# Output projection and down products as products of 64 rows in an attention and feed-forward kernel

## The chip, the cores and the metric

The kernel runs on one core of a Trainium2 chip. Its time is device microseconds for one execution; the median of several executions counts.

The engines are named as the profile names them: PE is TensorE's products, PEld its weight loads, DVE is VectorE, ACT is ScalarE, POOL is GpSimd, and SP is SyncE, which here issues nearly all DMAs.

## The reference

For 2048 tokens of width 576, an attention branch (32 heads of 18) is gated by a feed-forward branch (hidden width 4608):

```python
x = A_x                                         # 1 x 2048 x 576
xn = layernorm(x)
q, k, v = split_heads(xn @ wqkv)                # 32 heads of 18
s = softmax(q @ k.T * 18 ** -0.5) @ v @ wo
g = silu((gelu(xn @ w_gate) * (xn @ w_up)) @ w_down)
out = x + s * g
```

All inputs and the output are float32.

## The kernel before

**Precision.** Operands of the large products are split in a high and a low part (`split`), and a product is the sum of three: high by high, high by low, low by high.

**Stages.** A first stage normalizes and transposes x and projects q, k and v. The rest is one long loop of *sections*, 144 in all: the feed-forward branch goes over 4 blocks of 512 tokens (`b`), in each over 18 groups (`r`) of 2 x 128 hidden columns, and one section is one such set of 128 columns. Nine sections (`FIRST`) come before the attention proper, 128 run beside it (`ATT`), and the last seven after it.

**A section** (`section`, `gate_up`) has 27 pairs of products for the gate and the up projection. A pair is two products of 64 rows by 512 columns, one on the upper and one on the lower 64 rows of the array, into two banks, `pg` and `pu` (L388). Spread between them are 16 pairs of the attention, each with one product of scores (`pe`, L729) and one of the maxima that the softmax needs (`pm`, L698), on opposite halves as well. ACT takes the exponential of `pe` (L730), DVE reduces `pm` (L699).

**Behind a section** come, on PE in the order of the program text: the products with the values (`acc`, L764, 128 rows by 32 columns, 16 of them, which the profile shows as 32), sometimes a small transposition of the maxima (`max_end`, L712), a group of the output projection (`project_o`, L582, `po`, 14 products of 128 rows and 288 columns), and down products (`down`, L426, `py`, 128 rows and 288 columns, 6 to a result). `activate` makes the hidden values from `pg` and `pu` (L401 to L409), and `finish` splits them (`hh`, `hl`) and queues the group's down products in `FF["down"]` as two halves of 24, for token tiles 0, 1 and 2, 3. `downs` runs what is due. Inside the attention, both halves of most groups fall due together (`once`), as a run of 48 behind the next group's first section. DVE adds each result to `Y` (L432), or ACT copies it there in a block's first group (L430).

The output projection of a block is 8 groups, one every second section, always in front of a run of 48. DVE multiplies its result with the gate (L584), POOL adds x (L585), and SP stores it in the next section.

**Banks.** The 8 banks of PSUM go by tag: two `f` (`pg`, `pu`), three `m` (`pm`, `acc`, `po`), three `s` (`pe`, and `py` in turn).

**Order.** PE runs in the order of the text. The other engines' queues are ordered by a planner, save where `keep_in_program_order` pins an instruction. In the nine lead sections SP loads keys in chunks of 12 DMAs (`load_k`, L662), pinned, beside the weights of the next section (`load_gu`, L114), which POOL splits (`split_gu`, `wh` L94, `wl` L96).

Of the kernel before, what the change touches and what calls it, by code (L numbers as in the profile page):

```python
# [8 lines left out]
F32 = mybir.dt.float32  # L9
F32R = mybir.dt.float32r  # L10
AF = mybir.ActivationFunctionType
ALU = mybir.AluOpType
# [5 lines left out]
P = 128  # L18
# [19 lines left out]
G = 2  # L38
# [28 lines left out]
def kernel(ctx: ExitStack, tc: tile.TileContext, x, wqkv, wo, w_gate, w_up, w_down, out):  # L67
# [20 lines left out]
    identr = const.tile([P, P], F32R, name="identr")  # L88
    nc.gpsimd.tensor_copy(identr, ident)
    all_t = slice(0, TB)  # L90


    def split(hi, lo, raw, keep=lambda i: i):
# [47 lines left out]
    with tc.tile_pool(name="pro", bufs=1) as pro, tc.tile_pool(name="pps", bufs=1, space=PSUM) as pps:  # L141
# [156 lines left out]
        def after(what, before):  # L298
            tc.add_manual_dep(what.ins, before.ins.name, mybir.DependencyInfo(
                mybir.DependencyClass.Sync, mybir.DependencyReason.DATA), reason="VectorE alone on the first x")  # L300

        raw_v, ahead_qk, QR = [], [], []
        t = ORDER[0]
        c0 = slice(t * P, (t + 1) * P)
# [28 lines left out]
        for b in range(NB):  # L333
# [37 lines left out]
    ps = ctx.enter_context(tc.tile_pool(name="ps", bufs=1, space=PSUM, reuse_waits="tile"))  # L371


    FF = {"w": ahead, "xd": XD, "down": [], "gates": [], "n": 0,
          "Y": ffn.tile([P, TB // P, D], F32, name="Y")}
    finals = []

    def gate_up(tag):

# [32 lines left out]
            nc.vector.tensor_tensor(t1, t1, pu, op=ALU.mult)  # L412
        return t1

    def down(b, r, hs, wd, Y, js):
        for j in js:
            tt = slice(j * P, (j + 1) * P)
            for c in range(2):
                cc = slice(288 * c, 288 * c + 288)
                tag = "sf"[c if b == NB - 1 and r == NR - 1 else 0]  # L420
                py = ps.tile([P, 288], F32, name="py", tag=tag, bufs=BANKS[tag])
                n = 0
                for g in range(G):
                    hh, hl = hs[g]
                    for a, w in ((hh, wd[0]), (hh, wd[1]), (hl, wd[0])):
                        nc.tensor.matmul(py, a[:, tt], w[:, g, cc], start=(n == 0), stop=(n == 3 * G - 1))  # L426
                        n += 1
                yy = Y[:, j, cc]
                if r == 0:
                    nc.scalar.activation(yy, py, AF.Copy)  # L430
                else:
                    nc.vector.tensor_tensor(yy, py, yy, op=ALU.add)  # L432
                if b == NB - 1 and r == NR - 1:
                    finals.append((Y, j, c))
        if b < NB - 1 and r == NR - 1:
            FF["gates"] += [(b, j, c, Y) for j in js for c in range(2)]

# [44 lines left out]
        FF["act"] = activate(pg, pu, n < ATT.stop)  # L482

    def downs():
        while FF["down"] and (FF["down"][0][-1] < FF["n"] or FF["n"] == NF):
            down(*FF["down"].pop(0)[:-1])
            if FF["down"] and FF["gates"]:
                gates()

    def finish(pool=ffn, cut=split, bufs=1):  # L490

        n = FF["n"] - 1
        b, r = divmod(n // G, NR)
        hh = ffn.tile([P, TB], F32R, name="hh", bufs=G + 1)
        hl = ffn.tile([P, TB], F32R, name="hl", bufs=G + 1)
        cut(hh, hl, FF["act"])
        FF["hs"].append((hh, hl))
        if n % G == G - 1:
            wd = FF.pop("wd", None)
            if not wd:  # L500
                wd = [pool.tile([P, G, D], F32R, name=m, bufs=bufs) for m in ("dh", "dl")]
                cut(*wd, FF["rawd"])
            for h in range(2):
                once = n in ATT and n + G in ATT and r != NR - 2
                FF["down"].append((b, r, FF["hs"], wd, FF["Y"], (2 * h, 2 * h + 1), n + 1 + (0 if once else h)))
# [5 lines left out]
    OG = {}  # L511
    HIND = TB // P - 1

    def load_o(b, k, pool=op, heads=range(H)):
# [58 lines left out]
    def project_o(b, i, S2=None, o=None, ow=OW):  # L573
        c, j = divmod(i, TB // P)
        cc = place(b, i)[1]
        if b < NB - 1:
            xx, yy = OG["xy"]
        po = ps.tile([P, TB], F32, name="po", tag="m", bufs=3)
        o = o or OG["o"]
        terms = [(k, x, w) for k in range(KT) for x, w in ((0, 0), (0, 1), (1, 0))] + [(KT, 0, 0), (KT, 0, 1)]  # L580
        for m, (k, x, w) in enumerate(terms):
            nc.tensor.matmul(po[:, 0:288], o[x][:, k, :], ow[w][:, k, :], start=(m == 0), stop=(m == len(terms) - 1))  # L582
        if b < NB - 1:
            nc.vector.scalar_tensor_tensor(yy, yy, 0.25, po[:, 0:288], op0=ALU.mult, op1=ALU.mult)  # L584
            nc.gpsimd.tensor_tensor(yy, yy, xx, op=ALU.add)  # L585
            OG["y", b, i] = yy
        elif S2 is not None:
            nc.scalar.activation(S2[:, j], po[:, 0:288], AF.Copy)
        return po[:, 0:288]

# [10 lines left out]
    def tasks(n, part):  # L601
        for t in todo.pop((n, part), []):
            t()
# [37 lines left out]
    with tc.tile_pool(name="att", bufs=1, reuse_waits="tile") as att:  # L641
# [293 lines left out]
```

## Time and profile before

| | |
|---|---|
| median of 3 executions | 2584.83 us (2584.62 to 2585.79) |
| the profiled execution's own time | 2584.62 us |
| its span, first to last instruction | 2582.7 us |
| granted clock of TensorE | 1.000 |
| PE busy | 2575.9 us |
| DVE, ACT, POOL busy | 2010.5, 1502.5, 1389.8 us |
| products of py (L426) | 3 x 1152 |

Busy time of PE counts overlapping products once and holds their fill, so it does not say how close PE is to its best. The distance from the start of one product to the start of the next does; the chain in order of time gives it, since a piece in that chain lasts until the next piece begins. In the timeline a product's length is its time through the array (0.3 to 0.5 us), several times the distance to the next one.

### The profile page before, as it was taken

Reading aid. Unit: us, or ns where it says so; the run is one execution under the profiler, and the core shown is the slowest. Engines: PE = TensorE matmul, PEld = TensorE weight load, DVE = VectorE, ACT = ScalarE, POOL = GpSimd, SP = SyncE. Lnnn points to the kernel's source line nnn. Section 1 sums busy time; section 2 is a strip of 40 time slices with the busy share of each in tenths; the row PEclk is TensorE's granted clock in tenths of the full one; section 3 lists DMA queues with packets and bytes.
Section 4 is the critical chain, followed back from the end, with each engine's and each line's share of the span. In section 5 each row is a group of like instructions: output and inputs, shape, how many; then the busy total and the mean of one; then the engine's idle time right before and its main releaser. Section 6 shows DMA issues by size and latency. Waiting matters only on the chain.

```text
span 2582.7 us, 56466 instructions
## 1 busy us (share of the span) xinstructions
PE 2575.9 (100%) x20982; PEld 1959.8 (76%) x20982; DVE 2010.5 (78%) x3501; ACT 1502.5 (58%) x2715; POOL 1389.8 (54%) x1506
## 2 busy tenths in 40 slices
PE   9999999999999999999999999999999999999999
PEld 8888777777777777777777777777777777777778
DVE  5326888888887888888888888888888888888445
ACT  3223466666666666565667765556666765566642
POOL 2117554554566465556457565555455755555553
PEclk9999999999999999999999999999999999999999
DMA  8866443344455444544445444445445543545342
GB/s 265 267 237 162 117 104 98 102 105 105 105 135 131 110 114 105 136 111 113 127 114 133 119 125 112 125 112 133 108 109 126 141 114 104 139 110 137 78 117 59
DMA packets 394912, 326.93 MB, mean 127 GB/s; under 512 B 107980, under 2 KB 308684, under 8 KB 394640
## 3 DMA queue, kind: packets, MB, share of 16 engines
q1 hardware_dynamic: 394640, 323.32, 47.3%
q8 instruction: 168, 2.75, 0.5%
q14 instruction: 104, 0.85, 0.1%
HBM read 269.79 MB, written 52.88 MB: 125 GB/s over the span
## 4 chain that ended last, share of the span: by engine, by line
PE 99%; DVE 1%; DMA 0%; POOL 0%; ACT 0%; issue 0%; SPq 0%; DVEq 0%
PE pg L388 25%; PE py L426 18%; PE acc L764 18%; PE pu L388 10%; PE pe L729 9%; PE pm L698 9%; PE po L162 7%; PE po L582 2%; DVE mx L699 0%; PE pt L223 0%; PE pm L712 0%; DMA xx<-in_A_x_dram 0%; DVE bs L191 0%; POOL wh L94 0%; DVE m L706 0%
## 5 line engine op out<-in xcount | busy, mean ns | idle before, releaser
L730 ACT ACTIVATE pT<-pe 128x512 f32<-128x512 f32 x2048 | 1151.6, 599 | 678.4 <-PE pm L698 578.7
L699 DVE TENSOR_REDUCE mx<-pm 128x1 f32<-128x512 f32 x2048 | 1260.0, 683 | 76.4 <-PE pm L698 73.1
L388 PE MATMUL pg<-xd,wh 64*128 64x512 f32 x2592 | 935.5, 393 | 0.0
L388 PE MATMUL pu<-xd,wh 64*128 64x512 f32 x2592 | 935.1, 393 | 0.0
L698 PE MATMUL pm<-KS,q 64*128 64x512 f32 x2048 | 785.2, 388 | 0.2 <-DVE accs L770 0.2
L729 PE MATMUL pe<-q,KS 64*128 64x512 f32 x2048 | 777.9, 387 | 0.0
L94 POOL TENSOR_SCALAR wh<-raw 128x384 fp32r<-128x384 f32 x432 | 228.3, 529 | 610.2 <-PE pu L388 264.0
L388 PEld LDWEIGHTS pg<-xd,wh 64*128 64x128 f32 x2592 | 476.2, 184 | 98.5 <-issue 19.9
L388 PE MATMUL pg<-xd,wl 64*128 64x512 f32 x1296 | 502.0, 387 | 0.9 <-POOL wl L96 0.9
L388 PE MATMUL pu<-xd,wl 64*128 64x512 f32 x1296 | 501.8, 387 | 0.0
L388 PEld LDWEIGHTS pu<-xd,wh 64*128 64x128 f32 x2592 | 477.1, 184 | 22.6
L764 PE MATMUL acc<-pT,VS 128*32 128x512 f32 x4096 | 466.0, 595 | 0.0
L96 POOL TENSOR_TENSOR wl<-raw,wh 128x384 fp32r<-128x384 f32 x432 | 442.1, 1024 | 34.1
L698 PEld LDWEIGHTS pm<-KS,q 64*128 64x128 f32 x2048 | 375.7, 184 | 38.6 <-DVE mx L699 4.9
L729 PEld LDWEIGHTS pe<-q,KS 64*128 64x128 f32 x2048 | 370.1, 184 | 29.9
L432 DVE TENSOR_TENSOR Y<-py,Y 128x288 f32<-128x288 f32 x544 | 248.1, 457 | 161.1 <-PE py L426 160.8
L426 PE MATMUL py<-dh,hh 128*128 128x288 f32 x1152 | 346.0, 300 | 0.0
L426 PE MATMUL py<-dh,hl 128*128 128x288 f32 x1152 | 339.8, 295 | 0.0
L426 PE MATMUL py<-dl,hh 128*128 128x288 f32 x1152 | 339.6, 295 | 0.0
L764 PEld LDWEIGHTS acc<-pT,VS 128*32 128x32 f32 x4096 | 120.5, 109 | 274.5 <-issue 271.2
L388 PEld LDWEIGHTS pg<-xd,wl 64*128 64x128 f32 x1296 | 238.5, 184 | 31.7 <-POOL wl L96 1.2
L388 PEld LDWEIGHTS pu<-xd,wl 64*128 64x128 f32 x1296 | 238.7, 184 | 11.1
(127 smaller groups left out, 2946.5 us busy)
## 6 DMA issues: line engine op xcount, KB each, us to landing
KS<-qk SPq DMA_DIRECT2D x1536, 36.0 KB
raw<-in_B_w_gate_dram SPq DMA_DIRECT2D x144, 288.0 KB
raw<-in_B_w_up_dram SPq DMA_DIRECT2D x144, 288.0 KB
raw<-in_B_w_down_dram SPq DMA_DIRECT2D x68, 576.0 KB
VS<-vs SPq DMA_DIRECT2D x128, 152.0 KB
qk<-t SPq DMA_DIRECT2D x72, 256.0 KB
q<-qk SPq DMA_DIRECT2D x384, 36.0 KB
xd<-xhs SPq DMA_DIRECT2D x24, 384.0 KB
```

The lines of the kernel that those rows point to most:

```text
L94: first = nc.gpsimd.tensor_scalar(hi, raw, 1.0, 1.0, op0=ALU.mult, op1=ALU.mult)
L96: keep(nc.gpsimd.tensor_tensor(lo, raw, f(hi), op=ALU.subtract))
L162: nc.tensor.matmul(o, st, m, start=(i == 0), stop=(i == len(terms) - 1))
L388: nc.tensor.matmul(o, w[1 + wp][k][rr, c, :], xd[xp][k][rr, c, :], start=(i == 0), stop=(i == len(terms) - 1))
L426: nc.tensor.matmul(py, a[:, tt], w[:, g, cc], start=(n == 0), stop=(n == 3 * G - 1))
L432: nc.vector.tensor_tensor(yy, py, yy, op=ALU.add)
L582: nc.tensor.matmul(po[:, 0:288], o[x][:, k, :], ow[w][:, k, :], start=(m == 0), stop=(m == len(terms) - 1))
L698: nc.tensor.matmul(pm, QS[u, r][rr, t * P:(t + 1) * P], KS[(u * NA + c) % KB][r][rr, :], start=True, stop=True)
L699: nc.vector.tensor_reduce(MX[u][:, 2 * r + a, t, c:c + 1], pm, axis=AX.X, op=ALU.max)
L729: nc.tensor.matmul(pe, KS[(u * NA + c) % KB][r][rr, t * P:(t + 1) * P], QS[u, r][rr, :], start=True, stop=True)
L730: nc.scalar.activation(PT[u, kt][:, 2 * r + a, :], pe, AF.Exp, scale=SCALE)
L764: nc.tensor.matmul(ACC[u][32 * a:32 * a + 32, :], VS[(u * NA + c) % VB][:, v:v + 32], pt[:, a, :], start=first, stop=last, skip_group_chec ...
```

## The change

Three edits. A run of 48 down products becomes products of 64 rows: each product of 128 rows is cut in an upper and a lower half, and the halves of two results, in two banks, go as a pair. First one bank takes its lower and the other its upper halves, then they swap. Before the second half of a bank starts, a copy of one column on ACT (`behind`, on the tile `mark`) has waited for the last product of its first half. Results of the run take banks by the patterns `sfsf` and `smss`. Where a group of the output projection stands in front, `project_o` issues no products but hands them over, and `down_and_out` makes one row of the lot: lower halves in the order output projection, downs; upper halves in the order downs, output projection. The result of the group is then put at the end of that row. Runs in a block's first group (r = 0), and downs that do not go as 48, stay as they are. The third edit moves the loads of a chunk of keys in the lead sections: they begin behind section 2 instead of section 1.

```diff
+    def after(what, before):          # (moved up from the first stage, otherwise unchanged)
...
+    mark = const.tile([P, 1], F32, name="mark")
+    nc.vector.memset(mark, 0.0)
...
+    DOWN = [(a, w, g) for g in range(G) for a, w in ((0, 0), (0, 1), (1, 0))]
...
+    def down_product(py, hs, wd, j, c, i, rr=slice(0, P), start=False, stop=False):
+        a, w, g = DOWN[i]
+        return nc.tensor.matmul(py, hs[g][a][rr, j * P:(j + 1) * P], wd[w][rr, g, 288 * c:288 * c + 288],
+                                start=start, stop=stop)
+
+    def behind(one):
+        it = nc.scalar.activation(mark, mark, AF.Copy)
+        after(it, one)
+        return it
+
+    def down_and_out(b, r, hs, wd, Y, po):
+        bank_o, product_o, put_o = po
+        m = len(DOWN)
+        pys, seen = {}, {}
+
+        def downs_of(a):
+            for k, (j, c) in enumerate((j, c) for j in range(TB // P) for c in range(2)):
+                for i in range(m):
+                    def step(k=k, j=j, c=c, i=i):
+                        if a == 1 and i == 0:
+                            pys[k] = bank("sfsfssms"[k])
+                        one = down_product(pys[k], hs, wd, j, c, i, slice(HR * a, HR * a + HR), a == 1 and i == 0,
+                                           a == 0 and i == m - 1)
+                        if a == 0 and i == 0:
+                            after(one, seen[k])
+                        if i == m - 1:
+                            if a == 1:
+                                seen[k] = behind(one)
+                            else:
+                                add_down(b, r, pys[k], Y, j, c)
+                    yield step
+
+        def out_of(a):
+            for i in range(len(OUT)):
+                def step(i=i):
+                    product_o(bank_o, i, slice(HR * a, HR * a + HR), a == 0 and i == 0, a == 1 and i == len(OUT) - 1)
+                yield step
+
+        for lower, upper in zip([*out_of(0), *downs_of(0)], [*downs_of(1), *out_of(1)]):
+            lower()
+            upper()
+        put_o()
+
+    def down(b, r, hs, wd, Y, js, once):
+        last = len(DOWN) - 1
+        if once and r > 0 and not FF["po"]:
+            tags = ("sfsf", "smss")[js[0] // 2]
+            pys = {(j, c): bank(tags[2 * (j - js[0]) + c]) for j in js for c in range(2)}
+            seen = {}
+            for swap in range(2):
+                for j in js:
+                    for i in range(len(DOWN)):
+                        for a in range(2):
+                            c = a ^ swap
+                            one = down_product(pys[j, c], hs, wd, j, c, i, slice(HR * a, HR * a + HR),
+                                               swap == 0 and i == 0, swap == 1 and i == last)
+                            if swap == 1 and i == 0:
+                                after(one, seen[j])
+                    if swap == 0:
+                        seen[j] = behind(one)
+                    else:
+                        for c in range(2):
+                            add_down(b, r, pys[j, c], Y, j, c)
+        else:
...
     def downs():
+        if FF["po"] and FF["po"] is not True:
+            (b, r, hs, wd, Y, *_), _ = FF["down"].pop(0), FF["down"].pop(0)
+            down_and_out(b, r, hs, wd, Y, FF["po"])
...
     def project_o(b, i, S2=None, o=None, ow=OW):
...
+        due = FF["down"][0] if FF["down"] else None
+        if FF["po"] and due and due[1] > 0 and due[-2] and due[-1] < FF["n"]:
+            FF["po"] = po, product, put
+            return None
...
-            while n > 0 and chunk < KB and chunk * SLOTS <= slot + SLOTS:
+            while n > 1 and chunk < KB and chunk * SLOTS <= slot + SLOTS:
...
+            FF["po"] = (n, 1) in todo
             tasks(n, 1)
             downs()
+            FF["po"] = None
```

More of the change, by code (lines that the diff above doesn't have):

```diff
@@ L90 @@
     all_t = slice(0, TB)
+    def after(what, before):
+        tc.add_manual_dep(what.ins, before.ins.name, mybir.DependencyInfo(
+            mybir.DependencyClass.Sync, mybir.DependencyReason.DATA), reason="ordered by hand")
     def split(hi, lo, raw, keep=lambda i: i):
@@ L297 @@
         NQT = 2 * D // P
-        def after(what, before):
-            tc.add_manual_dep(what.ins, before.ins.name, mybir.DependencyInfo(
-                mybir.DependencyClass.Sync, mybir.DependencyReason.DATA), reason="VectorE alone on the first x")
         raw_v, ahead_qk, QR = [], [], []
@@ L413, in activate, with add_down @@
         return t1
[L415 to L434, printed above, removed]
+    def add_down(b, r, py, Y, j, c):
+        yy = Y[:, j, 288 * c:288 * c + 288]
+        if r == 0:
+            nc.scalar.activation(yy, py, AF.Copy)
+        else:
+            nc.vector.tensor_tensor(yy, py, yy, op=ALU.add)
+        if b == NB - 1 and r == NR - 1:
+            finals.append((Y, j, c))
@@ new lines, with bank @@
+    DOWN = [(a, w, g) for g in range(G) for a, w in ((0, 0), (0, 1), (1, 0))]
+    def bank(tag):
+        return ps.tile([P, 288], F32, name="py", tag=tag, bufs=BANKS[tag])
+    def down_product(py, hs, wd, j, c, i, rr=slice(0, P), start=False, stop=False):
[6 more added lines that the diff above has]
+        return it
@@ new lines, in down @@
+    def down(b, r, hs, wd, Y, js, once):
[18 more added lines that the diff above has]
+                            add_down(b, r, pys[j, c], Y, j, c)
+        else:
+            for j in js:
+                for c in range(2):
+                    py = bank("sf"[c if b == NB - 1 and r == NR - 1 else 0])
+                    for i in range(len(DOWN)):
+                        down_product(py, hs, wd, j, c, i, start=(i == 0), stop=(i == last))
+                    add_down(b, r, py, Y, j, c)
@@ L504, in finish @@
                 once = n in ATT and n + G in ATT and r != NR - 2
-                FF["down"].append((b, r, FF["hs"], wd, FF["Y"], (2 * h, 2 * h + 1), n + 1 + (0 if once else h)))
+                FF["down"].append((b, r, FF["hs"], wd, FF["Y"], (2 * h, 2 * h + 1), once, n + 1 + (0 if once else h)))
     op = ctx.enter_context(tc.tile_pool(name="op", bufs=1, reuse_waits="tile"))
@@ L511 @@
     OG = {}
+    OUT = [(k, x, w) for k in range(KT) for x, w in ((0, 0), (0, 1), (1, 0))] + [(KT, 0, 0), (KT, 0, 1)]
     HIND = TB // P - 1
@@ L577, in project_o, with product, put @@
             xx, yy = OG["xy"]
-        po = ps.tile([P, TB], F32, name="po", tag="m", bufs=3)
+        po = ps.tile([P, TB], F32, name="po", tag="m", bufs=3)[:, 0:288]
         o = o or OG["o"]
[L580 to L589, printed above, removed]
+        def product(po, i, rr=slice(0, P), start=False, stop=False):
+            k, x, w = OUT[i]
+            nc.tensor.matmul(po, o[x][rr, k, :], ow[w][rr, k, :], start=start, stop=stop)
+        def put():
+            if b < NB - 1:
+                nc.vector.scalar_tensor_tensor(yy, yy, 0.25, po, op0=ALU.mult, op1=ALU.mult)
+                nc.gpsimd.tensor_tensor(yy, yy, xx, op=ALU.add)
+                OG["y", b, i] = yy
+            elif S2 is not None:
+                nc.scalar.activation(S2[:, j], po, AF.Copy)
+        due = FF["down"][0] if FF["down"] else None
+        if FF["po"] and due and due[1] > 0 and due[-2] and due[-1] < FF["n"]:
+            FF["po"] = po, product, put
+            return None
+        for m in range(len(OUT)):
+            product(po, m, start=(m == 0), stop=(m == len(OUT) - 1))
+        put()
+        return po
     AB = NQ * NA
```

2 lines of the change are left out of this document (1 added, 1 removed).

## The prediction, made before the changed kernel had run

> **What bounds the kernel now.** First the page: who is busy, and which chain ended last.
>
> ```profile
> span 2582.7 us, 56466 instructions
> PE 2575.9 (100%) x20982; PEld 1959.8 (76%) x20982; DVE 2010.5 (78%) x3501; ACT 1502.5 (58%) x2715; POOL 1389.8 (54%) x1506
> PEclk9999999999999999999999999999999999999999
> PE 99%; DVE 1%; DMA 0%; POOL 0%; ACT 0%; issue 0%; SPq 0%; DVEq 0%
> ```
>
> TensorE (PE) is the whole chain at a full clock; every other engine has a fifth or more of the span free. So the change is worth what it takes from, or adds to, the steps of PE from product to product. Nothing else counts until it makes PE wait. A busy PE isn't a PE at its best, though, so the second view is the chain in order of time, around two of the runs that the change rewrites: one with a group of the output projection (po, L582) before the 48 down products (py, L426), one without.
>
> ```profile
> 1214.09 2.06 PE po L582 x14
> 1216.14 6.37 PE py L426 x48
> 1222.51 0.42 PE pg L388
> 1232.48 3.57 PE acc L764 x32
> ...
> 1236.23 0.42 PE pg L388
> ...
> 1249.77 6.57 PE py L426 x48
> 1256.34 0.42 PE pg L388
> 1256.77 0.23 PE pe L729
> ```
>
> Behind po the 48 products take 6.37 us, 132.7 ns each, and hide their weight loads. Where py itself follows acc, the same 48 take 0.20 us more; and the first pair of gate products behind either run takes 0.42 us where a pair takes 0.23. So a cost sits at each change of kind, on the way in and on the way out. The third view, PE in order of time, shows the way out product by product:
>
> ```profile
> 1222.08 0.29 PE L426 MATMUL py<-dl,hh 128*128 128x288 f32 x1
> 1222.21 0.29 PE L426 MATMUL py<-dh,hl 128*128 128x288 f32 x1
> 1222.44 0.49 PE L388 MATMUL pg<-xd,wh 64*128 64x512 f32 x1
> 1222.44 0.49 PE L388 MATMUL pu<-xd,wh 64*128 64x512 f32 x1
> 1222.78 0.39 PE L729 MATMUL pe<-q,KS 64*128 64x512 f32 x1
> 1222.78 0.39 PE L698 MATMUL pm<-KS,q 64*128 64x512 f32 x1
> 1223.01 0.39 PE L388 MATMUL pg<-xd,wl 64*128 64x512 f32 x1
> ```
>
> py to pg is 0.23 us where products of 128 rows follow each other at 0.133, and pg to pe is 0.34 where pairs of 64 rows follow at 0.23: 0.10 + 0.11 = 0.21 us for going from 128 rows to 64. Two facts matter for the change. Products of the upper and the lower 64 rows start in the same 0.01 us, so two halves cost one step. And pg to pe and pe to pg, all 64 rows, cost nothing at their borders.
>
> **The change part by part.**
>
> *How many.* By the code's condition for `once`, groups that end in the odd sections 9 to 133 go as a run of 48, without the three of r = 16: 60. The three of r = 0 (copied by ACT) keep 128 rows. That leaves 57 in halves: 24 with a po group in front (8 for each of the first three blocks), fused into one row of 14 + 48 = 62 pairs, and 33 alone as two calls of 24 pairs. Pairs of halves: 24 x 62 + 33 x 48 = 3072, as many as there were products.
>
> *Removed: one change of row count a run.* acc to halves stays a change of kind (where no downs stand between, the gate pairs behind acc pay the same 0.42, at 1236.23, as behind py). Halves to gate pairs is 64 rows to 64 rows, and I take its cost as that of pg to pe, none. 57 x 0.21 = 12.0 us less. The Trainium skill (TensorEngine Tiling (Array Packing), Key Properties) says that changing the tiling mode, not just the tile, drains TensorE; the 0.21 us above agrees, and by that rule two kinds of pairs in 64 x 128 tiles have no drain between them.
>
> *The step of a pair of 288 columns.* No row of this trace has 64 rows and 288 columns. The nearest rows: 132.7 ns for 128 rows and 288 columns (above); at 512 columns, 128 rows against 64:
>
> ```profile
> 29.83 12.60 PE po L162 x54
> 1222.44 0.18 PEld L388 LDWEIGHTS pg<-xd,wh 64*128 64x128 f32 x1 [0.16 <-issue]
> 1222.44 0.18 PEld L388 LDWEIGHTS pu<-xd,wh 64*128 64x128 f32 x1
> ```
>
> 12.60 / 54 = 233.3 ns for 128 rows. A section has 27 gate and 16 score pairs; from 1222.51 to 1232.48 that is 9.97 us, less 0.2 for its entry, by 43: 227.2 ns. So pairs of halves are 6.1 ns cheaper at 512 columns, and both loads of a pair start together. The bounds inside the likely case: 126.6 ns (the same 6.1 less) and 132.7 (no gain). I take 131, nearer to 132.7, since that row has the 288 columns and the other difference comes from another stage. 3072 x 1.7 ns = 5.2 us less (bounds 18.7 and 0; above 132.7 only by a limit that the rivals name).
>
> *The lead: the loads of keys that move one section later.* `n > 1` puts the 12 loads of the second chunk of keys behind the next weights on SP's queue. Now:
>
> ```profile
> 208.66 5.73 SPq L662 DMA_DIRECT2D KS<-qk  x12
> 214.50 0.62 SPq L114 DMA_DIRECT2D raw<-in_B_w_gate_dram  x1
> 215.16 0.64 SPq L114 DMA_DIRECT2D raw<-in_B_w_up_dram  x1
> 220.01 1.18 POOL wh L94 x2
> 221.19 0.97 POOL wl L96
> PEld pg L388 <- POOL wl L96: 1.2, 1, 1.2
> ```
>
> PE waits 1.2 us, once, for a split that waits for weights issued behind those 12. With the weights 5.7 us earlier the wait goes: 1.2 us less. What is late next: the keys are wanted some 4 us into that section, about 225; issued by 215 they are there. Bounds 0 and 1.2.
>
> *Added: the marks.* A bank may not take both halves at once, so the second half's first product waits for a tiny ACT copy that waits for the first half's last product. ACT does nothing in these runs:
>
> ```profile
> 1212.20 0.63 ACT L407 ACTIVATE t<-t 128x512 f32<-128x512 f32 x1 [0.26 <-DVE t L402]
> 1223.26 3.04 ACT L730 ACTIVATE pT<-pe 128x512 f32<-128x512 f32 x5 [10.44 <-PE pm L698]
> 1222.55 0.46 DVE L432 TENSOR_TENSOR Y<-py,Y 128x288 f32<-128x288 f32 x1 [0.34 <-PE py L426]
> 11.05 0.26 ACT L207 ACTIVATE xx<-xx 128x64 f32<-128x64 f32 x1 [0.23 <-DVE xx L205]
> ```
>
> The add at 1222.55 starts 0.34 us after the start of the product it waits for (1222.21); a mark starts as late, takes 0.26 (ACT's smallest copy), and I allow 0.05 back to PE: 0.65 us. Alone, six other pairs lie between: the waiting product comes 7 x 0.133 = 0.93 us after, its load 0.80. Fused, nine steps: 1.19. Cost nothing; behind a late mark PE's whole queue would stand. In 3 of the 33 (the last group of a block) four tanh of 0.44 us stand on ACT before the second call's marks; I put 0.4 us each there: 1.2 us more.
>
> *Moved: banks, adds, put.* The runs now take both f banks and one m bank. f was pg and pu, and its last reader in DVE is long done; an m bank is the oldest of three:
>
> ```profile
> 1212.08 0.68 DVE L406 TENSOR_TENSOR t<-t,pg 128x512 f32<-128x512 f32 x1
> 1214.23 0.69 DVE L770 TENSOR_TENSOR accs<-acc,accs 128x512 f32<-128x512 f32 x1 [0.67 <-PE acc L764]
> 1223.24 1.34 DVE L699 TENSOR_REDUCE mx<-pm 128x1 f32<-128x512 f32 x2 [0.23 <-PE pm L698]
> ```
>
> The third row's reduces start 0.80 into the section that began at 1222.44. L406 ends at 1212.76, the run begins at 1214.09: 1.3 us of cover. At the end two adds follow the last pair (fused: one add and the put of po): 0.34 + 2 x 0.46 = 1.26 us after the last product, 1.13 into the section, so the first mx is 0.3 us late. The last banks that these adds free are wanted by the section's third score pair; with the first at 0.34 and 16 in 9.97 us, that is about 1.6 in. Cost nothing; without that cover up to 0.3 us a run. The sum yy + xx on POOL, the store on SP and POOL's next split of oh, which must wait for the last product that reads it, come the run's 6.4 us later, and POOL's next splits of weights may stand behind them:
>
> ```profile
> 1226.48 0.52 POOL L94 TENSOR_SCALAR wh<-raw 128x384 fp32r<-128x384 f32 x1
> 1227.08 1.01 POOL L96 TENSOR_TENSOR wl<-raw,wh 128x384 fp32r<-128x384 f32 x1
> ```
>
> These are the next weights behind such a run, done at 1228.1; no section uses them before 1236.23. Even the whole 6.4 us is within the 8.1 that cover it: nothing.
>
> *Sum.* -12.0 - 5.2 - 1.2 + 1.2 = -17.2 us. The profiled execution took 2584.62 (span 2582.7 and 1.9 around it), 0.21 under the median 2584.83; from the median: **2567.6 us**.
>
> **The rivals.**
>
> *1: PE can't be fed halves that fast (slower).* A pair is four instructions, two loads and two products; in 132.7 ns that is 33 ns each. The fastest stretch of loads and products in the trace is the transposes:
>
> ```profile
> 9.60 2.17 PEld L223 LDWEIGHTS pt<-ident,xx 128*128 128x128 f32 x20 [0.68 <-DVE xx L205]
> ```
>
> (2.17 - 0.19) / 19 = 0.104 us for a load and a product, 52 ns each; gate pairs need 227 / 4 = 57. If 52 were the limit, a pair would take 208 ns: 3072 x 75 ns = +231 us, and with the other terms about 2803 us. It decides from 136.6 ns a pair on, where 3072 x 3.9 ns eat the 12.0. Against it: transposes load 128 columns and stream 128, which may be their own bound, and a pair's four instructions start in 0.01 us, so a queue is kept ahead of the array; it only has to last. The Trainium skill (TensorE: Matmul & The Clock Gate, Part 1, "Wait — 56ns, not 53.3ns?") gives about 25 ns as the least from start to start and 62 ns a product where the sequencer decodes in software; as an estimate from that page, four times 25 is 100 ns, which fits and leaves the sum as it is, and two products and two loads at 62 would be 248 ns, 354 us more. No run here shows which. 12%.
>
> *2: a wait takes the switch's place.* If a mark comes back 0.2 us later than worked out, or the adds at the end hold the first banks of the section, a run loses what it gained: 57 x 0.2 = 11.4 us back, about 2579 us. For it: only 0.15 us of margin at the load in the 33. Against: the rows above. 10%.
>
> *3: the switch stays.* If a drain comes with another column count or with both halves of a bank, the change does not do what it says: -5.2 and the lead alone, 2579.6; without the cheaper pair 2584.8. Against it: acc apart, no border between kinds of 64 rows costs anything. 6%.
>
> **How the numbers follow.** The forecast has 72%. About 0.2% (5.2 us) can be told from no change. Faster by more: the forecast, and most of rivals 2 and 3 where they end under 2579.6: 0.78. Within: the rest of those, 0.07. Slower: rival 1, and waits larger than the gain: 0.15. The likely case alone spans 2553 (pairs at 126.6) to 2574 (no cheaper pair, lead unchanged). The range is 2555 to 2583, which takes in most of rivals 2 and 3 and leaves out rival 1.
>
> **What would show it.** Chain in order of time: behind a run in halves the first gate pair at 0.23 instead of 0.42; a fused row of 62 pairs in about 8.3 us with its entry, 48 alone in about 6.5; no wait for wl near 220. Wrong: pairs of py over 137 ns (rival 1), waits of PE for mark, Y or yy with 0.1 us or more each (2), 0.42 still behind the runs (3).

## The result, and the profile after

The change made the kernel slower: 2597.6 us (median of 5 executions, 2595.43 to 2599.45) against 2584.69 (2584.52 to 2585.79) on the same chip, ratio 1.0048 with a 95% interval of 1.0033 to 1.0063. The profiled execution took 2598.2 us, its span 13.0 us more than before. The forecast was 2567.6.

From the page of the changed kernel, the span, the busy times, and the shares of the chain that ended last:

```profile
span 2595.7 us, 63232 instructions
...
PE 2583.0 (100%) x24054; PEld 1970.5 (76%) x24054; DVE 1984.0 (76%) x3502; ACT 1568.7 (60%) x3039; POOL 1397.8 (54%) x1506
...
PE 96%; DVE 1%; DMA 1%; POOL 1%; issue 0%; SPq 0%; ACT 0%; POOLq 0%; ACTq 0%; DVEq 0%
```

There are 3072 products more, as counted. PE is still nearly the whole chain, but its share fell from 99% to 96%, and POOL and DMA, at 0% before, now have 1% each. That is the first sign that another engine ended a wait.

The chain in order of time, at the same two runs as before the change (start, length, what):

```profile
1225.36 4.64 PE py L433 x68
...
1231.73 0.23 PE pg L390
1231.96 0.23 PE pe L815
...
1255.22 3.57 PE acc L850 x32
1258.80 6.94 PE py L433 x89
1265.74 0.11 PE pg L390
1265.85 0.13 PE pu L390
1265.97 0.26 PE pe L815
```

Behind the fused row (first two lines) the first gate pair takes 0.23 us where it took 0.42: the change of row count is gone. Behind the lone run it is otherwise: the run itself is no shorter, and pg and pu, one pair, stand in the chain one behind the other. The timeline shows why, first inside that run, then at its end:

```profile
1262.68 0.30 PE L433 MATMUL py<-dh,hl 64*128 64x288 f32 x2
1262.81 0.68 PE L433 MATMUL py<-dh,hh 64*128 64x288 f32 x2
1263.09 0.18 PEld L433 LDWEIGHTS py<-dh,hh 64*128 64x128 f32 x1 [0.23 <-DVE Y L422]
1263.46 0.29 PE L433 MATMUL py<-dh,hh 64*128 64x288 f32 x1
1263.46 0.29 PE L433 MATMUL py<-dh,hl 64*128 64x288 f32 x1
...
1264.86 1.61 DVE L422 TENSOR_TENSOR Y<-py,Y 128x288 f32<-128x288 f32 x4 [1.83 <-PE py L433]
...
1265.45 0.39 PE L390 MATMUL pg<-xd,wh 64*128 64x512 f32 x1
1265.58 0.39 PE L390 MATMUL pu<-xd,wh 64*128 64x512 f32 x1
1265.74 0.18 PEld L815 LDWEIGHTS pe<-q,KS 64*128 64x128 f32 x1
```

```profile
PEld py L433 <- DVE Y L422: 7.5, 33, 0.2
...
PEld py L433 <- POOL hh L98: 5.7, 2, 4.5
```

The second fence is the view of waits (waited for: us in all, times, longest). In each of the 33 lone runs the upper half of the last token block's first pair waits 0.23 us for a DVE add. The code says which: the banks of the second call are `smss`, and the fourth of them is the `s` bank that held the third result of the first call, whose add is not done. The lower half does not wait. So the pair is split (0.68 us for two products that start 0.28 apart), and from there the halves run one product out of step: at 1263.46 the lower is at hl while the upper is at hh. They leave the run so, and the section begins with pg 0.13 us ahead of pu. Its first score product (pe) waits as well: its load starts at 1265.74, 0.05 us after one of the run's last adds ends.

The last line of that view is a second loss, at two places only. Around the first of them, the run of r = 0 near 797 us, on POOL, SP and PE (the number in brackets is the idle time before, with what ended it):

```profile
777.88 1.16 POOL L98 TENSOR_SCALAR dh<-raw 128x1152 fp32r<-128x1152 f32 x1
782.92 1.29 POOL L610 TENSOR_TENSOR OT<-OT,den 128x512 f32<-128x512 f32 x1 [3.89 <-DMA den<-rT]
784.18 3.13 POOL L100 TENSOR_TENSOR dl<-raw,dh 128x1152 fp32r<-128x1152 f32 x1
...
793.83 0.51 POOL L98 TENSOR_SCALAR wh<-raw 128x384 fp32r<-128x384 f32 x1 [4.94 <-DMA q<-zq]
...
802.02 0.61 POOL L98 TENSOR_SCALAR hh<-t 128x512 fp32r<-128x512 f32 x1
...
787.34 0.67 SPq L118 DMA_DIRECT2D raw<-in_B_w_gate_dram  x1
...
798.16 0.29 PE L433 MATMUL py<-dh,hl 128*128 128x288 f32 x1
802.69 0.61 PE L433 MATMUL py<-dh,hh 128*128 128x288 f32 x1 [4.23 <-POOL hh L98]
...
804.44 0.44 PE L433 MATMUL py<-dh,hh 128*128 128x288 f32 x1
804.68 0.44 PE L433 MATMUL py<-dl,hh 128*128 128x288 f32 x1
```

The kernel before, same stretch (its run of r = 0 begins at 795.38):

```profile
775.26 2.67 POOL L96 TENSOR_TENSOR dl<-raw,dh 128x1152 fp32r<-128x1152 f32 x1
...
782.37 1.29 POOL L535 TENSOR_TENSOR OT<-OT,den 128x512 f32<-128x512 f32 x1 [2.87 <-DMA den<-rT]
...
792.24 0.61 POOL L94 TENSOR_SCALAR hh<-t 128x512 fp32r<-128x512 f32 x1
...
778.54 0.66 SPq L114 DMA_DIRECT2D raw<-in_B_w_gate_dram  x1
```

Before, POOL split the down weights (dh, dl) and then waited for den, the sums of the softmax that OT is divided by. Afterwards the planner has put OT between dh and dl, so the same wait stands in front of dl. dl frees the raw buffer, so SP issues the next gate weights at 787.34 and not at 778.54; their split, then four gate products (th), then the split of hh follow on POOL. hh is split 9.8 us later than before, for a run that begins 2.4 us later (797.79), and PE stands 4.23 us. No line that the change touches runs there: the run of r = 0 keeps its 128 rows.

The wait costs more than its length. Busy time of the engines by stretches, the granted clock in the column behind POOL's entry:

```profile
790.00:800.00 10.00, 8.45 (x73) 4.57 (x71) 7.86 (x13) 6.07 (x11) 6.00 (x9) 1.00 0.55 124
800.00:806.00 6.00, 2.81 (x10) 2.47 (x11) 0.00 (x0) 0.41 (x1) 5.38 (x8) 0.60 0.53 156
806.00:812.00 6.00, 6.00 (x39) 5.84 (x39) 0.00 (x0) 2.56 (x7) 2.69 (x4) 0.83 0.88 223
```

Behind it the granted clock falls: 0.60 and 0.83 in two stretches of 6 us make 6.8 us at half clock, and products of 128 rows follow each other at 0.24 us (804.44, 804.68) where they took 0.133. By these shares the half clock lasts from about 801.2 to 808.0, and PE works from 802.69 on. The waits of 4.23 us for hh and 0.50 us for hl, and half of the 4.8 us that PE then works at half clock, make 7.1 us; the run takes 13.94 us and not 6.57, 7.4 more. The Trainium skill (TensorE: Matmul & The Clock Gate, Part 1, "What's actually happening") says that about 3.4 us without work put the array on half clock and that as long a stretch of work brings it back. This trace agrees in that the wait of 4.23 us is longer than that; but the half clock lasted twice that stretch, and shorter waits had the same effect, as the end of this document tells. Where they differ, the measurement decides.

The second place is the lone run at 2404, 9.05 us instead of 6.73, with a like chain on POOL. Here OT and its wait of 11.97 us stand in front of both dh and dl:

```profile
2375.69 1.30 POOL L610 TENSOR_TENSOR OT<-OT,den 128x512 f32<-128x512 f32 x1 [11.97 <-DMA den<-rT]
...
2382.39 2.67 POOL L100 TENSOR_TENSOR dl<-raw,dh 128x1152 fp32r<-128x1152 f32 x1
...
2401.50 0.51 POOL L98 TENSOR_SCALAR wh<-raw 128x384 fp32r<-128x384 f32 x1 [14.87 <-DMA raw<-in_B_w_up_dram]
...
2405.18 0.63 POOL L98 TENSOR_SCALAR hh<-t 128x512 fp32r<-128x512 f32 x1
```

The kernel before, where this run begins at 2394.06, 10.2 us earlier:

```profile
2371.08 0.65 SPq L114 DMA_DIRECT2D raw<-in_B_w_gate_dram  x1
...
2393.69 0.62 POOL L94 TENSOR_SCALAR hh<-t 128x512 fp32r<-128x512 f32 x1 [1.40 <-DVE t L409]
```

There no division stood in front of dl, which was split at 2368.38. In the changed kernel dl is split 14.0 us later, and the gate weights that SP issues behind it start at 2389.09, 18.0 us later.

### The profile page after: what moved, and what is told of

The parts are those of the page before. It is cut to its first block, busy times and chain, and to the rows that moved or that the text cites. A ratio compares the mean times of both kernels' runs of the same rounds, so it can differ in the third digit from the quotient of the medians.

```text
span 2595.7 us, 63232 instructions
## 1 busy us (share of the span) xinstructions
PE 2583.0 (100%) x24054; PEld 1970.5 (76%) x24054; DVE 1984.0 (76%) x3502; ACT 1568.7 (60%) x3039; POOL 1397.8 (54%) x1506
## 4 chain that ended last, share of the span: by engine, by line
PE 96%; DVE 1%; DMA 1%; POOL 1%; issue 0%; SPq 0%; ACT 0%; POOLq 0%; ACTq 0%; DVEq 0%
PE pg L390 24%; PE py L433 18%; PE acc L850 17%; PE pu L390 10%; PE pe L815 9%; PE pm L784 9%; PE po L166 7%; PE po L658 2%; DVE mx L785 1%; DMA raw<-in_B_w_up_dram 0%; PE pt L227 0%; PE pm L798 0%; DMA raw<-in_B_w_gate_dram 0%; DMA xx<-in_A_x_dram 0%; POOL hl L100 0%
## 5 line engine op out<-in xcount | busy, mean ns | idle before, releaser
L98 POOL TENSOR_SCALAR wh<-raw 128x384 fp32r<-128x384 f32 x432 | 238.3, 553 | 528.5 <-DMA raw<-in_B_w_up_dram 231.2
L433 PE MATMUL py<-dh,hh 64*128 64x288 f32 (+1 forms) x2064 | 440.3, 300 | 5.2 <-POOL hh L98 5.2
L433 PE MATMUL py<-dl,hh 64*128 64x288 f32 (+1 forms) x2064 | 426.5, 294 | 0.0
L433 PE MATMUL py<-dh,hl 64*128 64x288 f32 (+1 forms) x2064 | 423.4, 293 | 1.3 <-POOL hl L100 1.3
L422 DVE TENSOR_TENSOR Y<-py,Y 128x288 f32<-128x288 f32 x544 | 233.8, 454 | 239.8 <-PE py L433 231.4
L433 PEld LDWEIGHTS py<-dh,hh 64*128 64x128 f32 (+1 forms) x2064 | 301.9, 185 | 52.8 <-issue 36.8
L433 PEld LDWEIGHTS py<-dh,hl 64*128 64x128 f32 (+1 forms) x2064 | 300.7, 185 | 1.9 <-POOL hl L100 1.9
```

The costliest lines, as they stand in the source:

```text
L98: first = nc.gpsimd.tensor_scalar(hi, raw, 1.0, 1.0, op0=ALU.mult, op1=ALU.mult)
L433: return nc.tensor.matmul(py, hs[g][a][rr, j * P:(j + 1) * P], wd[w][rr, g, 288 * c:288 * c + 288], start=start, stop=stop)
```

## The experiments

Two theories of the loss behind the lone runs were set against each other at first, called A and B in the expectations: that the halves come out of step by the wait for a bank and the section pays for that (A), or that the late adds hold the section's first banks (B). Three more (S and T; O and P) came with the results. Each kernel was timed beside the kernel before on the same chip (its medians there were 2584.7 to 2585.0 us).

**A free bank for the last result (banks).**

```diff
-            tags = ("sfsf", "smss")[js[0] // 2]
+            tags = ("sfsf", "smsm")[js[0] // 2]
```

> Changed kernel, but in the second call of a lone run the last result goes to a third m bank instead of the s bank that the first call's third result held (banks smsm for smss). Theory A (a wait of the second member of pair 31 for that bank's add on DVE, 0.28 us a run, leaves the two halves one product out of step, and that costs about 0.19 us more at the start of the next section): the step of 0.28 us after pair 30 goes, lone runs fall from 6.73 to 6.46 us, the sections behind them from 10.05-10.12 to 9.87; 29 lone runs x 0.45 = 13 us less, about 2585 us, with the two single stalls at the 797 us and 2404 us runs (7.4 and 2.5 us) still there. Theory B (the next section's loss comes from the late adds that hold its first banks): lone runs fall to 6.46 too, but the sections stay at 10.05 or more: about 2590 us.

Measured: 2587.9 us, ratio 1.0009 (1.0000 to 1.0018). The wait for Y is gone; the 29 ordinary lone runs take 6.47 us (0.10 under the kernel before, 0.26 under the changed one), and a full section behind them 9.88 us (10.07 on average in the changed kernel, 9.98 before). That is what A expected, but it does not refute B: by the rotation of the three `s` banks the same edit also gives the section's first score product a bank that has long been free. wait_both and one_waits below part the two. The long waits stayed, and the second grew (runs of 14.16 and 14.74 us in the profile; 13.94 and 9.05 in the changed kernel).

**The other order of taking the banks (late_first).**

```diff
-pys = {(j, c): bank(...) for j in js for c in range(2)}
+pys = {(j, c): bank(...) for j in js for c in ((0, 1), (1, 0))[j == 3]}
```

> Changed kernel with the two s banks of the last token tile swapped, so that the first member of pair 31, not the second, has the bank that comes free last; the wait itself stays. Theory A: both halves wait together and stay in step: lone runs 6.55 to 6.65 us (the wait of 0.1 to 0.2 remains), sections behind them 9.87, about 2588 us. Theory B (late adds hold the next section's banks): sections stay at 10.05 to 10.12, at least 2593 us.

Measured: 2599.0 us, 1.0054 (1.0041 to 1.0066). The expectation missed: lone runs, sections and the 33 waits of 7.5 us in all are those of the changed kernel, and the half that waits is the same. So the edit did not do what it was meant to (why is not known), and it says nothing of the theories.

**The fused rows alone (fused_only):** lone runs at 128 rows again (`if False and once and ...`).

> Changed kernel with the 33 lone runs in 128 rows as before; the 24 fused rows and the moved loads of keys stay. Theory A: each fused row and its next section keep their 0.19 us, 24 x 0.19 + 1.2 = 5.8 us less than before; the stall at the 797 us run, which needs the marks in the run that closes a block, is gone; the one near 2404 us, which comes from POOL and SP orders after the last fused row, stays (2.5 us): about 2581 us. Rival C (fused rows disturb POOL and SP more widely): 2585 us or more.

Measured: 2585.9 us, 1.0001 (0.9992 to 1.0009). The fused rows bring their 4.55 us (run 0.09, section 0.10, 24 times) and the lead its 1.2, but single waits for splits of POOL take most of it: 2.1 us in the run near 2394, 1.1 and 1.0 in two runs of r = 0. The profiled execution took 2583.0 us; what the slower ones among the eleven, up to 2587.8, lose besides is not shown. No edit is made at these places; the order on POOL moved again.

**A version picked by its order on POOL (best_try):** free bank, the runs that close a block at 128 rows (`0 < r < NR - 1`), the last two po groups of the third block not fused (`n < 117`).

> Banks smsm as in the first of these, and the changed parts are left out where the orders of POOL and SP went wrong: the three lone runs that close a block stay in 128 rows, and the last two groups of the output projection of the third block are not fused. Theory A: 22 fused rows x 0.19, 32 lone runs x 0.21 less one switch each for the two behind an unfused group, and 1.2 for the lead, no single stalls: about 2573 us. Theory B: sections behind lone runs stay at 10.05: about 2578 us. If the single stalls have another cause than the order of POOL, they stay and it is 2580 us or more.

Measured: 2579.7 us, 0.9978 (0.9969 to 0.9987), under both kernels. Its lone runs behave as in banks. It is about 7 us above A's number, and the trace puts most of that down to single losses of 0.6 to 2.3 us at five places: three runs, by waits for hh and hl, and two sections, by waits for an add of DVE (accs).

**Every division put later (pin, banks_pin, inner_pin):** all `norm_o` but the last two of a block stand behind `finish()`, one section later, and are ordered behind the last split; in the changed kernel, with the free bank, and with the closing runs at 128 rows as well.

```diff
-  at(*((t0 + 2 - last, 2) if k < KT - 1 else (t0 + 1, 0)), norm_o, k)
+  at(*((t0 + 3 - last, 3) if k < KT - 1 else (t0 + 1, 0)), norm_o, k)   # part 3: behind finish()
...
+  it = nc.gpsimd.tensor_tensor(OT[0:n, k, :], ..., op=ALU.mult)         # as before, but named
+  tc.add_manual_dep(it.ins, SPLIT["lo"].ins.name, ...)                  # order alone: behind the last low part
```

> The changed kernel with one thing added: each division of the attention's output by its sums (OT<-OT,den on POOL) is put one section later and behind the last split that POOL has queued, so that it never stands between dh and dl. Theory O: the 7.4 us of the run of r = 0 near 797 and the 2.5 us of the run near 2404 come from POOL waiting for den in front of dl; both go, 2597.6 - 9.9 = about 2588, the run of r = 0 takes 6.6 us again and no product waits over 2 us for hh; the granted clock stays at full. Rival P: the late weights come from SP's queue (stores behind the fused rows) and the order on POOL only shows it; then the stalls stay or move to other runs, about 2597. The 30 other lone runs keep their +0.16 and +0.09 us under both.

> The same order on POOL, and the last bank of the second call taken from m and not s (smsm). Both edits together undo both losses, if they are independent: the lone runs 0.2 us a run under the kernel before (-6.9 us), the fused ones -4.6, the lead -1.2, three runs at the end of a block +1.1, no stall: 2585 - 11.6 = about 2573. If the stalls have a cause besides den, about 2580 or more.

> As the run before, and the three runs that close a block (marks behind four tanh on ACT) stay in products of 128 rows: 1.1 us less if those runs cost their +0.38 us by the marks, about 2572; 2573 if it makes no difference.

Measured: 2593.4 (1.0031, 1.0020 to 1.0043), 2579.95 (0.9981, 0.9973 to 0.9990) and 2582.05 us (0.9988, 0.9980 to 0.9997). The wait near 2404 is gone, the one at the run of r = 0 is not: 12.86, 11.36 and 11.39 us; in inner_pin a second such run takes 10.54 us. The cause had moved to SP. There is one den buffer; with the division a section later its load waits until the division before is done, and the weights stand behind it in SP's queue (in pin den at 782.80, raw at 785.23 for a run at 797.50). So O held at 2404 alone, and P's stores are not what stood in front of the weights, but the load of den: the edit repaired POOL and broke SP.

**Both halves wait (wait_both), one half waits alone (one_waits).** What does the section behind a lone run pay for? In wait_both, on the changed kernel, the lower half waits for the same add:

```diff
+  if swap == 0 and i == 0 and a == 0 and j == 3:
+      after(one, FF["add", 1, 0])          # the add that the upper half waits for
```

> The changed kernel, order on POOL as it is, with one wait more: in the second call of a lone run the first product of the lower half on the last token block also waits for the add that the upper half waits for, so that both halves wait together. Theory S (a wait of one half alone leaves the halves a product out of step to the end of the run, and the section behind pays for it): the steps of 281 and 239 ns become one long step, the run keeps about +0.16 to +0.2 us, and the section behind goes from 10.02-10.05 to 9.87 us: 33 x 0.19 = 6 us less than 2597.6, about 2592. Rival T (the section pays for the bank that the last adds still hold): the section stays at 10.05 us and the time at 2597 or above.

In one_waits the bank is free (smsm), and the upper half (`a == 1`) is made to wait for that add all the same:

> The kernel with the free bank (smsm), and in the second call of each lone run the upper half alone is made to wait, on the last token block, for the add it waited for in the changed kernel; the bank that the section's first score pair takes stays long free. It parts the two costs. Theory T: the section behind pays for the bank that the adds of the run still hold, not for halves out of step; the run goes from 6.47 back to 6.73 us, the section stays at 9.88: 2587.9 + 33 x 0.26 = about 2596.5. Theory S: halves that leave the run out of step cost the section the 0.19 us as well: section 10.02 to 10.07, about 2603.

Measured: wait_both 2602.2 us (1.0066, 1.0052 to 1.0079), one_waits 2594.9 (1.0039, 1.0025 to 1.0053). Theory S falls in wait_both: the halves come out of the run in step (pg and pu 3 ns apart behind the run at 1261.54), yet the section takes 10.07 us on average, as in the changed kernel. The run did not keep its length, as the expectation had it: it takes 6.86 us and not 6.73, which is 4 of the 4.6 us that wait_both lies above the changed kernel. The waits show another cause for the section:

```profile
PEld pe L817 <- DVE Y L422: 6.8, 31, 0.2
```

The section's first score product takes the `s` bank that the second call began with, and the adds of the run hold it. In the changed kernel the view of waits names this wait only 3 times, but the load starts at the same moment, 0.05 us after the add. In banks no such wait is left. But T alone does not hold either: in one_waits that bank is free, the run takes 6.73 us, and the section 9.97, just between 9.88 and 10.07. Halves out of step cost the section 0.10 us without any wait of its own; a bank held too long makes it 0.18 to 0.20, with or without them.

**Two divisions moved (banks_one, after_one).** With and without the free bank, only the two divisions that had made the long waits are ordered behind the split:

```diff
+  if (b == 0 and k == 2) or (last and k == 0):
+      at(t0 + 2, 3, norm_o, k, True)       # behind finish() and its split
+  else:
       at(*((t0 + 2 - last, 2) if k < KT - 1 else (t0 + 1, 0)), norm_o, k)
```

> The kernel with the free bank (smsm), and two divisions OT<-OT,den alone put behind the down weights' split in front of which they stood: the one near 780 us and the one near 2370. If their place on POOL is what makes the two long waits (run of r = 0 near 795: +7.6, run near 2394: +8.2), both go: 2587.9 - 15.8 = about 2572, and the clock shows no dip. If the r = 0 run only shows a chain that has no slack left (weights, 8 gate products, split of hh), a wait of 1 to 5 us stays there: about 2575.

> The changed kernel (last bank of s, smss) with the two divisions OT<-OT,den put behind the split, as in the run before (2574.6 with the free bank). If bank and order are separate costs that add up: the run of r = 0 takes 6.57 us, no clock dip, the lone runs keep +0.16 and +0.09 us, so 2597.6 - 7.4 - 2.5 and some tenths = about 2587; against 2574.6 the bank is then 33 x 0.45 less the waits it hid = 12 to 15 us. If the stalls come from the bank (a later run pushes the chain on POOL back), they stay: 2597.

Measured: banks_one **2574.56 us** (2574.30 to 2574.86), 0.9961 (0.9948 to 0.9973), the best version of all; after_one 2588.2, 1.0014 (1.0005 to 1.0023). The two differ in the bank alone; their queues on POOL and SP hold the same instructions in the same order. Both have no long wait, the run of r = 0 takes 6.57 us, and the clock stays at full. POOL and the chain in banks_one:

```profile
773.73 2.67 POOL L102 TENSOR_TENSOR dl<-raw,dh 128x1152 fp32r<-128x1152 f32 x1
...
790.44 0.62 POOL L100 TENSOR_SCALAR hh<-t 128x512 fp32r<-128x512 f32 x1
```

```profile
1245.00 6.56 PE py L436 x88
1251.56 0.23 PE pu L393
1251.79 0.00 PE pg L393
1251.80 0.23 PE pm L793
```

hh and hl are split by 792.4, and the run of r = 0 begins at 792.9. And behind the lone run the first gate pair takes 0.23 us, as behind a fused row, with pg and pu together. The four kernels make a square:

| | order as the planner left it | two divisions moved |
|---|---|---|
| bank taken early (smss) | 2597.6 | 2588.2 |
| free bank (smsm) | 2587.9 | 2574.56 |

The bank costs 9.7 or 13.6 us, the order 9.4 or 13.3, each by the row or column in which the other stands. Where PE's time went, from the starts of all products in the profiled executions (us against the kernel before; the profiled execution of banks, 2592.0 us, was the longest of its eleven):

| | changed | after_one | banks | banks_one |
|---|---|---|---|---|
| 24 fused rows and the sections behind | -4.55 | -4.55 | -4.55 | -4.55 |
| 33 lone runs | +8.25 | +6.01 | +6.29 | -1.95 |
| the sections behind them | +2.92 | +2.96 | -3.51 | -3.59 |
| three runs of r = 0 | +7.37 | 0.00 | +8.42 | 0.00 |
| the section at 220 us | -1.22 | -1.23 | -1.23 | -1.22 |
| all the rest | +0.22 | +0.12 | +1.48 | +1.23 |
| sum | +12.99 | +3.31 | +6.90 | -10.08 |

**Gate products moved (banks_g, inner117_g).** The four pairs of th on POOL in front of the split of hh that the run of r = 0 waits for are moved a section ahead (`gates()` behind `finish()`), in banks and in best_try:

> The kernel with the free bank (smsm), and the last four pairs of gate products on POOL (th, 4.7 us), which stand in front of the split of hh that the run of r = 0 waits for, put behind the split of the section before; the order of OT is as it comes. If the run of r = 0 waits because POOL's chain to hh has no slack, its wait goes (-7.6) and the one near 2394 stays: about 2580.5. If only OT in front of dl counts, and its order stays, no change: 2588.

> The best kernel so far (2579.7: smsm, the runs that close a block at 128 rows, the last two groups of the third block not fused), with the same move of four pairs of gate products. Its runs of r = 0 waited 0.6 and 1.4 us: about 2578 if the move takes these away, 2579.7 if it does nothing.

Measured: 2584.3 (0.9999, 0.9991 to 1.0008) and 2583.3 us (0.9995, 0.9986 to 1.0004). In banks_g the runs of r = 0 take 6.57 us again, but now th stands in front of dl, the weights come later, and the section ahead of each of these runs waits (+4.0, +2.0, +1.2 us); the run near 2394 still takes 10.78 us. In inner117_g that loses more than was there to gain. The chain weights, th, hh has no slack to move things in.

**The closing runs at 128 rows (inner_one), the lead alone (lead_only).** inner_one is banks_one with `0 < r < NR - 1`; lead_only is the kernel before with `n > 1`.

> Free bank, the two divisions behind the split, and the three runs that close a block left at 128 rows. Those runs take 6.96 us in halves and 6.57 us in 128 rows, their section 0.1 us less in halves: 3 x 0.29 = 0.9 us less than 2574.6, about 2573.7, if the order on POOL around them stays harmless; some us more if it makes a new wait.

> The kernel before, with the loads of the second chunk of keys one section later alone (n > 1). The wait of 1.2 us for wl near 220 goes, nothing else moves: 2584.7 - 1.2 = 2583.5. Rival: the order of the planner shifts elsewhere and gives it back, 2584 to 2586.

Measured: inner_one 2578.4 us (0.9980, 0.9971 to 0.9989), 4 us above banks_one. The three runs are 0.39 us shorter, but the order around them moved again: three other runs are 2.0, 1.1 and 0.8 us longer. lead_only 2583.95 (0.9995, 0.9986 to 1.0004), 1.0 us under its neighbour; the section at 220 us is 1.19 us shorter, one run of r = 0 near 2040 us is 0.43 longer, and little else moves. The time alone could not tell that from nothing, the trace does.

## Why the prediction was wrong, step by step

**The switch of row count, -12.0: right, and nearly in size.** In banks_one a fused row and its section are 0.19 us shorter, an ordinary lone run and its section 0.10 + 0.11 = 0.21; over all 57, without the marks, that is 11.6 us. Behind a fused row of halves the steps from py to pg and from pg to pe are 133 and 233 ns; behind 128 rows they were 225 and 337. The rule on draining (the Trainium skill, TensorEngine Tiling (Array Packing), Key Properties) was read rightly for pairs of one tile shape. Rival 3 is refuted.

**The cheaper pair, -5.2: wrong by its whole size.** The steps of halves average 132.7 ns (129 to 141) in fused rows, as those of 128 rows do (132.7). The 6.1 ns that were carried over from 512 columns are not there at 288. The bound 132.7 was the value to take: its row had the 288 columns. Rival 1 is refuted by the same number: four instructions fit into 132 ns.

**The lead, -1.2: right,** by the trace of lead_only (-1.19).

**The marks: right for the 54 other runs, and about right for the three that close a block.** Those are 0.39 us longer than 128 rows where the others are 0.10 shorter, and in banks_one PE waits for the mark there (0.7 us in three waits). That is 1.5 us in all; 1.2 was put in.

**"Moved: banks, adds, put", with "Cost nothing": this is the first step that failed.** It asked who had used a bank before the run and who would want it behind. It did not follow the tags through the two calls of one run: the last of `smss` is the last `s` of `sfsf`, and its add runs 4 us into the run, which makes the run 0.26 us longer than in banks. And it gave the banks that the last adds free to the section's third score pair; by the rotation the first pair takes one that an add has just left or still holds, 0.19 us in the section. The price of both is 9.7 to 13.6 us.

**"Even the whole 6.4 us is within the 8.1 that cover it: nothing": the second.** The working moved one row's POOL and SP steps by the run's length and kept every queue's order. But the planner drew POOL's order anew, at places that the diff does not touch (how it comes to its order no run shows). At two of them a step that waits for a DMA came to stand in front of a split that frees a buffer. The cover there was not 8.1 us: before the change hl was split at 794.22, 1.2 us ahead of the run that needs it. The price is 9.4 to 13.3 us.

**The rivals.** Rival 2 had the right kind, a wait in place of the switch, and its own sign showed (waits for Y of over 0.1 us). It even named the adds that hold the first banks of the section. But it put one wait of 0.2 us on a run, where a lone run paid twice, 0.26 us for its own bank and 0.19 for the section's: 33 x 0.45 = 14.9 us, more than the 12.0 of the switch. That an order could turn was no rival at all. So the slower side was left at 0.15, for rival 1, which did not come, and for waits larger than the gain, to which no size was given.

**The sum put right.** -17.2, and 5.2 for the pair: -12.0. banks_one, without the two failed steps, is 10.1 under the kernel before; 1.2 us of the other 1.9 us lie in the rest of the table, in stretches that the change does not touch, 0.4 in the switch (11.6 for 12.0) and 0.3 in the marks (1.5 for 1.2). The bank's 13.6 and the order's 9.4 on top lead back to the changed kernel's +12.9; that is the square read along one side, no second measurement.

## What to carry to other kernels

When a loop body is cut in two calls, write down which bank each result gets, through both calls and into the work behind, with the time at which its reader is done; a wait of 0.23 us that held one half of a pair of products cost the run 0.26 us, and the section behind another 0.10, because the halves went on out of step (one_waits). Where a planner orders an engine's queue, an edit in one place can change the order far from it, as in fused_only and inner_one: compare the queues before explaining a wait, and pin the steps that wait for a DMA behind those that free a buffer. A single wait on TensorE may be charged twice, as at 798 us here: once as a wait and once as half clock.

## What the runs showed of the hardware

- The length of a wait did not decide alone whether the half clock came, nor for how long. In banks_pin PE waited 1.93 and then 0.82 us for hh and hl, and the granted clock in the two stretches of 3 us behind was 0.73 and 0.70, which makes 3.4 us at half clock. In inner_pin 1.09 and 0.82 us (the run at 1417) were enough for 3.4 us too, and in pin 2.32 and 0.79 us were followed by 6.8 us, as much as behind the 4.23 us of the changed kernel. But in one_waits 1.92 and 0.82 us (the run at 2401), and in inner117_g 2.2 us in a section, left the clock at full.
- Halves out of step don't fall back into step by themselves: after one wait of 0.23 us the two row halves stay a product apart for the last 17 pairs of the run, and in one_waits, where the section's first bank is free, they stay so through the whole section behind (0.12 us apart at its last pair), which takes 9.97 us and not 9.88.
- The executions of banks, with its two long waits, scatter from 2583.8 to 2592.0 us (eleven), those of banks_one, without them, from 2574.3 to 2574.9 (five). That the waits are the reason is not shown: the kernel before scatters from 2583.6 to 2588.2 without a long wait (twenty-one, beside banks_one).
